# A long convolution by transforms, then token mixing: another pitch for x in SBUF, joint spectrum products, and two copies on another engine

## The chip, the cores and the metric

The kernel runs on one core of a Trainium2 chip. A core has five engines that each work through a queue of their own, in order: PE (TensorE, matrix products; its weight loads are listed apart as PEld), DVE (VectorE), ACT (ScalarE), POOL (GpSimd) and SP (SyncE, here only DMA issues). They meet through semaphores. SBUF is the on-chip memory of 128 partitions, PSUM holds the results of PE, and 16 DMA engines move data between SBUF and the device memory. The metric is the device time of one execution in microseconds (us).

## The reference

The input x has 8 batches of 5696 tokens and 128 channels. Each channel is convolved along the tokens with a filter h of full length (by a transform of twice the length), and the result goes through a mixing block.

```python
# first block: B, S, D = 8, 5696, 128
L = 2 * S
Xf = np.fft.rfft(x, n=L, axis=1)
Hf = np.fft.rfft(h, n=L, axis=0)
y = np.fft.irfft(Xf * Hf[None], n=L, axis=1)[:, :S, :]
# second block, x is now y
theta = x @ w_theta
zr, zi = x * np.cos(theta), x * np.sin(theta)
y = einsum('ts,bsd->btd', w_tok_r, zr) + einsum('ts,bsd->btd', w_tok_i, zi)
u = x + y
out = u + np.maximum(u @ w_ch, 0.0)
```

## The kernel before

The second block, the mixing with two 5696 x 5696 matrices (matmuls of L1099 and L1020, matrices streamed in by POOL at L509 and transposed by VectorE at L714), takes the larger part of the run. The change touches the first block, the transform part, lines 82 to 366.

**The transform.** The length 11392 is split as N1 x N2 = 178 x 64. Of the 178 first frequencies K1 = 90 are kept. A sequence is laid out with its NB = 89 blocks of 64 tokens on the partitions. The work goes in eight groups: a pair of batches (bp = 0 to 3, e = 0, 1 inside the pair) and a half of the channels (dh = 0, 1; HD = 64 channels). Each group passes four stages:

- Stage a (`stage_a`, L185): for each channel one matmul (L194) with the 89 x 128 slice of x as the weights (128 = two batches x 64 tokens of the block) and the table f1_t, 180 columns, as the moving operand. Four channels share one PSUM tile; a copy to SBUF follows (L201, on ScalarE; for the filter h also L199, on VectorE). 16 chunks.
- Stage b (`stage_b`, L294, with `f2`, L204): for 8 frequencies at a time the second transform (L212, 32 small matmuls), a copy of the result from PSUM to xs (L310, ScalarE), and the product with the filter's spectrum hs, which SP loads four chunks ahead (L303). The spectrum's two parts (r = 0, 1) give two VectorE instructions (L312), one into u_t and one into v_t. 12 chunks, the last with 2 frequencies. At the end of `f2` for the last chunk stand 12 further matmuls (L218), whose results are not used.
- Stage c (`stage_c`, L318): the first inverse transform, 16 chunks of 8 channels, 16 matmuls each (L328 with weights from u_t, L329 from v_t), then a copy with a sign (L336 on VectorE, or L333 and L334 on ScalarE).
- Stage d (`stage_d`, L339): the last inverse transform, 7 chunks (six of 10 of the 64 token positions, one of 4) of L351 matmuls, then a copy to yt (L354, ScalarE), which SP stores.

**The order.** The instructions are written out in one order, and each engine takes its own in that order. `woven` sorts the chunks of several lists by a position between 0 and 1. For each group g there are two such stretches: stage c of g woven with stage a of g + 1, where stage a lies in the first 0.35 (g even) or 0.55 (g odd); then stage b of g + 1 woven with stage d of g.

**Buffers.** All PSUM tiles of the transform come from one pool of four (`psum`, L97). xs has two buffers, hs four, and x16, u_t, v_t, the result of stage a (a_), of stage c (g_) and yt have one each. u_t and v_t also hold the raw h and the filter's spectrum before group 0.

**The load of x.** `load_x` (L124) loads a pair of batches, float32 to float16, in 16 DMAs from POOL: 2 batches x 4 quarters of the 64 positions x the partitions 0 to 79 and 80 to 88. The first call stands in the setup, among the tables that POOL prepares (L150, L152). The others stand at the end of stage a's list for dh = 1 (`next_x`): with one x16 buffer, the first DMA waits until that stage's last matmul has read the old x. At most 8 DMAs of POOL are under way at a time.

The weights of L194 are `x16[:NB, :, dh * HD + q]`: 128 elements of 2 bytes, one per (batch, position), whose distance is the pitch of a row of x16, 128 elements or 256 B. For h the rows are 64 elements (`h16`, L118) and the distance 128 B. For u_t, v_t and g_ the 128 elements lie side by side.

Of the kernel before, what the change touches and what calls it, by code (L numbers as in the profile page):

```python
# [12 lines left out]
F16 = mybir.dt.float16  # L13
add = mybir.AluOpType.add
mult = mybir.AluOpType.mult
AF = mybir.ActivationFunctionType
# [6 lines left out]
def kernel(  # L23
# [10 lines left out]
    nc = tc.nc  # L34
    B, S, D = x.shape
    assert D == 128
    P = 128
# [39 lines left out]
    N2 = 64  # L77
    N1 = NF // N2
    NB = S // N2
    K1 = N1 // 2 + 1  # L80
    CK = 8
    HD = D // 2
    EN = N2 // 2 + 1
    WARM = 12
    assert N1 * N2 == NF and NB * N2 == S and NB % 2 == 1 and K1 <= P
    CHK = [(c0, min(CK, K1 - c0)) for c0 in range(0, K1, CK)]
    NCK = len(CHK)
    CN = 10
    CHN = [(c0, min(CN, N2 - c0)) for c0 in range(0, N2, CN)]
    UVW = 2 * HD * K1  # L90
# [6 lines left out]
    def psum():  # L97
        return fp.tile([P, 2, 512], F32, tag="ps", name="ps")
# [3 lines left out]
    def pool(name, bufs, stack, **kw):  # L102
        return stack.enter_context(tc.tile_pool(name=name, bufs=bufs, **kw))
# [3 lines left out]
    fx = pool("fft_x", 1, xin)  # L107
    NE, WB, BT = 9, 6 * 4 * CJ * 64, 7 * 1024
    keep = pool("keep", 1, ctx, side="right")
    fc = pool("fft_c", 1, conv, side="right")  # L110
# [1 line left out]
    s1 = pool("set_1", 1, setup, side="right")  # L112
    s2 = pool("set_2", 2, setup, side="right")

    u_t = fc.tile([P, UVW + P], F16)
    v_t = fc.tile([P, UVW + P], F16)
    uv = [t[:, :UVW].rearrange("p (e d k) -> p e d k", e=2, k=K1) for t in (u_t, v_t)]
    h16 = s1.tile([P, 2, N2, HD], F16)  # L118
    for p0, p1 in ((0, 80), (80, NB)):
        nc.gpsimd.dma_start(u_t[p0:p1, :N2 * D],  # L120
                            bass.AP(tensor=h.tensor, offset=h.offset + p0 * N2 * D,
                                    ap=[[N2 * D, p1 - p0], [1, N2 * D]]))

    def load_x(bp):  # L124
        x16 = fx.tile([P, 2, N2, D], F16, tag="x16", name="x16")
        for e in range(2):
            src = x[2 * bp + e]
            for n0 in range(0, N2, 16):
                for p0, p1 in ((0, 80), (80, NB)):
                    nc.gpsimd.dma_start(  # L130
                        x16[p0:p1, e, n0:n0 + 16, :].rearrange("p n d -> p (n d)"),
                        bass.AP(tensor=src.tensor, offset=src.offset + (p0 * N2 + n0) * D,
                                ap=[[N2 * D, p1 - p0], [1, 16 * D]]))
        return x16

    lane = fc.tile([P, 2], F32)
# [6 lines left out]
    def turns_of(pattern, base, lanes, m, per, quarter=None):  # L143

        n = 1
        for _, c in pattern:
            n *= c
        t = s2.tile([P, 11 * NB], F32, tag="turn", name="turn")[:m, :n]
        k = s2.tile([P, 11 * NB], F32, tag="whole", name="whole")[:m, :n]
        nc.gpsimd.iota(k, pattern=pattern, base=base, channel_multiplier=0,  # L150
                       allow_small_or_imprecise_dtypes=True)
        nc.gpsimd.tensor_scalar(t, k, lanes, 1.0 / per, op0=mult, op1=mult)  # L152
        if quarter is not None:
            quarter(t)
        nc.vector.tensor_scalar(k, t, MAGIC, None, op0=add)
        nc.vector.scalar_tensor_tensor(t, k, MAGIC, t, op0=ALU.subtract, op1=ALU.subtract)
        return t, k
# [12 lines left out]
    t, k = turns_of([[1, K1]], 0, lane[:NB, 1:2], NB, N1)  # L170
# [33 lines left out]
    def f2(a_st, c):  # L204
# [11 lines left out]
        if c == NCK - 1:  # L216
            for n in range(WARM):
                nc.tensor.matmul(ps[:, n % 2, ck * HD:ck * HD + 384], w_t2[:, 2, :P],  # L218
# [11 lines left out]
    for k0 in (0, 15, 30):  # L230
        w_table(k0)
    nc.vector.tensor_copy(h16[:NB], u_t[:NB, :N2 * D].rearrange("p (n h d) -> p h n d", h=2, d=HD))
    x16s = {0: load_x(0)}
    steps, a_h = stage_a(lambda q: h16[:NB].rearrange("p h n d -> p (h n) d")[:, :, q], True)
    woven(steps, [lambda k0=k0: w_table(k0) for k0 in range(45, K1, 15)])
# [20 lines left out]

    for c in range(NCK):
        h_chunk(c)
    nc.gpsimd.memset(u_t[:, UVW:], 0.0)
    nc.gpsimd.memset(v_t[:, UVW:], 0.0)  # L260

    r_u = fc.tile([P, P], F16)
    r_v = fc.tile([P, P], F16)
# [30 lines left out]
    def stage_b(a_st, dh):  # L294

        hs_of = {}

        def load(c):
            if c >= NCK:
                return  # L300
            hs = hs_of[c] = fh.tile([P, 2, HD * CK], F16, tag="hs", name="hs")
            for e in range(2):
                nc.sync.dma_start(hs[64 * e:64 * e + 64], hf_hbm[dh, c])  # L303

        def chunk(c):
            c0, ck = CHK[c]
            hv = hs_of[c].rearrange("p r (d k) -> p r d k", k=CK)
            ps = f2(a_st, c)
            xs = fs.tile([P, 2, HD, CK], F16, tag="xs", name="xs")
            nc.scalar.activation(xs[:, :, :, :ck], ps, AF.Copy)  # L310
            for r in range(2):
                nc.vector.tensor_tensor(  # L312
                    uv[r][:, :, :, c0:c0 + ck], xs[:, :, :, :ck],
                    hv[:, r:r + 1, :, :ck].to_broadcast([P, 2, HD, ck]), op=mult)
            load(c + LEAD)
        return [lambda c=c: load(c) for c in range(LEAD)], [lambda c=c: chunk(c) for c in range(NCK)]
# [22 lines left out]
    def stage_d(st, bp, dh, then=None):  # L339
        def chunk(n0, cn):  # L340
            if n0 == 0:
                st["yt"] = fg.tile([P, NB, N2], BF16, tag="yt", name="yt")
            g_, yt = st["g"], st["yt"]
            ps = psum()
            nq = 5 if cn == CN else cn
            for j in range(cn):
                n = n0 + j
                o = ps[:, j // nq, (j % nq) * NB:(j % nq + 1) * NB]
                for ri in range(2):
                    e_ = e_t[:K1, n, ri, :] if n < EN else e_t[:K1, N2 - n, ri, ::-1]  # L350
                    nc.tensor.matmul(o, g_[:K1, ri * N2 + n, :], e_, start=(ri == 0), stop=(ri == 1))  # L351
            y_out = yt[:, :, n0:n0 + cn].rearrange("p m (a q) -> p m a q", q=nq)
            y_in = ps[:, :cn // nq, :nq * NB].rearrange("p a (q m) -> p m a q", q=nq)
            nc.scalar.activation(y_out, y_in, AF.Copy)  # L354
            if n0 + cn == N2:
                if then is not None:
                    then(yt)
                if then is not None:
                    gate = nc.gpsimd.tensor_copy(small(0, 1)[HD:HD + 1], sides["phases"][1][HD:HD + 1, 3, H - 1:H]).ins
                for e in range(2):  # L360
                    t0 = H if then else 0
                    with tc.issue_after(gate) if then else ExitStack():
                        (nc.gpsimd if then else nc.sync).dma_start(
                            yt_hbm[dh * HD:(dh + 1) * HD, 2 * bp + e, t0:],
                            yt[64 * e:64 * e + 64].rearrange("p m n -> p (m n)")[:, t0:])
        return [lambda n0=n0, cn=cn: chunk(n0, cn) for n0, cn in CHN]
# [125 lines left out]
    def small(at, n):  # L492
        return ring["all"][:, WB + BT + at:WB + BT + at + n]
# [436 lines left out]
    for i, (k, p, tt, j0, s0, nj) in enumerate(stretches):  # L930
# [38 lines left out]
        if tt is None:  # L969
# [24 lines left out]
            if end_of_pair:  # L994
# [5 lines left out]
                c, c0 = c_last  # L1000
# [161 lines left out]
```

## Time and profile before

| | us |
|---|---|
| median of three runs | 2101.3 (2100.75 to 2103.45) |
| span of the profiled execution | 2098.1 |
| busy PE, DVE, ACT, POOL | 1979.5, 1595.2, 675.3, 912.5 |
| weight loads (PEld) | 1109.4 |
| first stage a of a group, first copy | 55.3 |
| stage c of the eight groups, first VectorE copy | 90.5, 132.4, 174.5, 217.7, 259.8, 304.4, 347.7, 394.6 |
| loads of x for the second to fourth pair, first issue | 100.0, 184.8, 270.1 |

The profile is of one execution, taken by the hardware profiler; times in it are microseconds from the span's start unless marked ns. The groups view gives for each line, engine and kind of instruction: the tiles, output <- inputs with partitions x elements, the count, then the busy time and the mean of one in ns, then the engine's idle time just before and what ended most of it. The timeline gives start, duration, engine, line, and how many are merged in the row (xN). In the windows view each row is a stretch of time with each engine's busy time. PEclk is TensorE's granted clock as a share of the full one. The ends of matmuls are modelled, so that the distance of their starts says more than their duration.

### The profile page before, as it was taken

What the parts mean: (1) busy time and instruction counts of PE and PEld (TensorE: products, weight loads), DVE (VectorE), ACT (ScalarE), POOL (GpSimd) and SP (SyncE); (2) the same over time, 40 slices, a digit from 0 to 9 for tenths busy, and PEclk for the clock granted to TensorE, in tenths of its full rate; (3) what the DMA queues carried; (4) which work ended last, traced back from release to release, by engine and by line L of the source; (5) the groups of instructions that cost most, each with busy time, mean ns of one, the idle gap of its engine ahead of it and who ended that gap; (6) DMA issues with size and microseconds to landing.
All of it is one profiled execution on the core that took longest, in us unless ns stands there. A gap on an engine that the chain in (4) does not pass through costs nothing.

```text
span 2098.1 us, 41505 instructions
## 1 busy us (share of the span) xinstructions
PE 1979.5 (94%) x15688; PEld 1109.4 (53%) x15865; DVE 1595.2 (76%) x2881; ACT 675.3 (32%) x995; POOL 912.5 (43%) x1662
## 2 busy tenths in 40 slices
PE   4888999878999999999999999899999999999998
PEld 3788888754444444444444444344444444444444
DVE  7777776776878888888886766886777777777867
ACT  5887877874332333333310000011111111111111
POOL 5301010327444636354557554435354545445450
PEclk8799999989999999999999999999999999999999
DMA  7357474989989989898999989869797887879693
GB/s 144 94 137 175 123 171 121 239 243 239 179 153 179 178 175 168 171 173 177 171 175 152 154 167 284 136 107 156 127 154 132 148 142 136 154 130 155 126 155 89
DMA packets 408233, 334.97 MB, mean 160 GB/s; under 512 B 85895, under 2 KB 358407, under 8 KB 407047
## 3 DMA queue, kind: packets, MB, share of 16 engines
q0 software_dynamic: 225952, 156.72, 52.8%
q1 hardware_dynamic: 176096, 164.05, 27.3%
q10 hardware_dynamic: 5984, 11.54, 1.6%
q8 instruction: 124, 2.03, 0.4%
q14 instruction: 77, 0.63, 0.1%
HBM read 377.11 MB, written 92.49 MB: 224 GB/s over the span
## 4 chain that ended last, share of the span: by engine, by line
PE 63%; DVE 4%; DMA 2%; issue 2%; POOL 0%; ACT 0%; DVEq 0%
PE m L1099 59%; DVE c L1106 2%; DMA ring<-in_moe_w_tok_r_dram 1%; DVE b L655 1%; PE v L801 1%; PE utp L794 1%; PE m L1103 1%; DVE wt L714 1%; PE tpz L742 0%; PE theta_ps L396 0%; POOL ring L509 0%; PE m L986 0%; DMA yT<-yt_hbm 0%; PE m L1020 0%; DMA zl<-zl_hbm 0%
## 5 line engine op out<-in xcount | busy, mean ns | idle before, releaser
L509 POOL DMA_DIRECT2D ring<-in_moe_w_tok_i_dram x720 | 390.8, 557 | 653.0 <-DVE wt L714 579.6
L509 POOL DMA_DIRECT2D ring<-in_moe_w_tok_r_dram x720 | 389.0, 559 | 145.8 <-DVE wt L714 85.5
L714 DVE STREAM_TRANSPOSE wt<-ring 128x384 f32<-128x384 f32 (+2 forms) x720 | 359.3, 523 | 110.3 <-PE m L1099 70.0
L1099 PE MATMUL m<-b,wt 128*128 128x512 bf16 x1599 | 385.9, 380 | 4.1 <-DVE wt L714 1.7
L1099 PEld LDWEIGHTS <-wt 128*128 128x128 bf16 x1804 | 176.4, 98 | 219.7 <-DVE wt L714 7.8
L1106 DVE TENSOR_TENSOR c<-c,m 128x512 f32<-128x512 f32 x412 | 265.2, 669 | 0.4 <-PE m L1099 0.4
L796 ACT ACTIVATE ring<-utp 128x512 bf16<-128x512 bf16 x85 | 50.8, 597 | 582.3 <-PE utp L794 582.3
L328 PE MATMUL ps<-r_u,u_t 128*128 128x128 f16 x1024 | 126.4, 223 | 6.4 <-ACT red L419 3.0
L329 PE MATMUL ps<-r_v,v_t 128*128 128x128 f16 x1024 | 125.5, 223 | 0.4
L1020 PE MATMUL m<-b,wt 128*128 128x512 bf16 x466 | 110.2, 381 | 8.9 <-DMA b<-z_hbm 4.9
L791 ACT ACTIVATE ub<-c 128x512 bf16<-128x512 f32 x88 | 55.0, 628 | 191.5 <-DMA ring<-in_moe_w_tok_r_dram 113.0
L130 POOL DMA_DIRECT2D x<-in_x_dram x64 | 33.9, 536 | 184.9 <-PE ps L194 174.8
L328 PEld LDWEIGHTS <-u_t 128*128 128x128 f16 x1024 | 103.4, 101 | 5.5 <-DVE u_t L312 4.6
L329 PEld LDWEIGHTS <-v_t 128*128 128x128 f16 x1024 | 102.4, 100 | 4.4 <-issue 2.4
L310 ACT ACTIVATE xs<-ps 128x1024 f16<-128x1024 f32 x96 | 96.6, 1030 | 14.7 <-DVE v_t L312 6.7
L312 DVE TENSOR_TENSOR u_t<-xs,hs 128x1024 f16<-128x1024 f16 x96 | 68.6, 715 | 29.2 <-ACT xs L310 19.0
L1020 PEld LDWEIGHTS <-wt 128*128 128x128 bf16 x528 | 51.1, 99 | 69.2 <-issue 9.6
L194 PE MATMUL ps<-f_t,x 89*128 89x180 f16 x512 | 77.2, 298 | 4.0 <-ACT xs L310 2.6
L212 PEld LDWEIGHTS <-w_t 64*128 64x128 f16 x3240 | 60.8, 102 | 37.5 <-issue 24.5
L398 ACT ACTIVATE red<-theta_ps,magic 128x512 f32<-128x512 f32 (+1 forms) x46 | 31.6, 687 | 134.6 <-PE theta_ps L396 104.5
L194 PEld LDWEIGHTS <-x 89*128 89x128 f16 x512 | 70.8, 241 | 5.5 <-issue 4.5
L744 ACT ACTIVATE ring<-tpz 128x512 bf16<-128x512 bf16 (+1 forms) x46 | 27.5, 597 | 131.9 <-PE tpz L742 113.0
(2895 smaller groups left out, 3868.9 us busy)
## 6 DMA issues: line engine op xcount, KB each, us to landing
ring<-in_moe_w_tok_r_dram POOLq DMA_DIRECT2D x352, 96.0 KB, 4.5
ring<-in_moe_w_tok_i_dram POOLq DMA_DIRECT2D x352, 96.0 KB, 4.9
ring<-in_moe_w_tok_r_dram POOLq DMA_DIRECT2D x352, 80.0 KB, 4.5
ring<-in_moe_w_tok_i_dram POOLq DMA_DIRECT2D x352, 80.0 KB, 3.9
hs<-hf_hbm SPq DMA_DIRECT2D x192, 128.0 KB, 3.1
cp_hbm<-c SPq DMA_DIRECT2D x88, 256.0 KB, 2.5
c<-cp_hbm SPq DMA_DIRECT2D x88, 256.0 KB, 4.4
out_dram<-c SPq DMA_DIRECT2D x88, 256.0 KB, 4.5
```

Source lines behind the costliest of these rows:

```text
L194: nc.tensor.matmul(ps[:, i // 2, (i % 2) * 2 * K1:(i % 2 + 1) * 2 * K1], lhs(q + i), f1_t[:NB], start=True, stop=True)
L212: nc.tensor.matmul(ps[:, e, j * HD:(j + 1) * HD], w_t2[rows, c0 + j, N2 * (1 - ri):N2 * (3 - ri)], a_st["a"][rows, ri * K1 + c0 + j, :], s ...
L310: nc.scalar.activation(xs[:, :, :, :ck], ps, AF.Copy)
L312: nc.vector.tensor_tensor(uv[r][:, :, :, c0:c0 + ck], xs[:, :, :, :ck], hv[:, r:r + 1, :, :ck].to_broadcast([P, 2, HD, ck]), op=mult)
L328: nc.tensor.matmul(o, u_t[:, at:at + P], r_u, start=True, stop=False)
L329: nc.tensor.matmul(o, v_t[:, at:at + P], r_v, start=False, stop=True)
L509: nc.gpsimd.dma_start(wb[32 * i:32 * i + 32, :ng, :nj * 64], bass.AP(tensor=a.tensor, offset=a.offset + row0 * S + p * H + i * QR + j0 * 6 ...
L714: nc.vector.transpose(wt.rearrange("p j t r -> p (j t r)").bitcast(F32).rearrange("p (j g t) -> p g j t", j=TJ, g=4)[:, :ng, :nj], wb[:, : ...
L791: nc.scalar.activation(ub[:m].rearrange("p b d -> p (b d)"), c[:m], AF.Copy)
L1020: nc.tensor.matmul(ms[n // 2 * 2 + h], a[n][:, j, :, r], bts_of[p][jj][n % 2 * 2 + h][:, r, :], start=(n % 2 == 0 and jj == 0 and r == 0), ...
L1099: nc.tensor.matmul(ms[q], a[q][:, j, :, r], bts[jj][q][:, r, :], start=(jj == 0 and r == 0), stop=(jj == NJ - 1 and r == 1 and q not in left))
L1106: nc.vector.tensor_tensor(c, z, ms[q], op=op)
```

## The change

Three edits:

- The rows of x16 get a pitch XP = 132 elements (264 B) of which 128 are used. The DMAs write them as 16 pieces of 128 elements per partition where they wrote one run of 2048.
- u_t and v_t become two parts of one tile uv_t, u_t in front, v_t behind it, without the 128 spare columns between them. The two products of a chunk with 8 frequencies become one instruction over (r, e, channel, frequency) in which xs is repeated over r and the spectrum over e. The last chunk, with 2 frequencies, keeps two instructions. One of two memsets of spare columns goes.
- In stage d the copies of the first and the fourth of seven chunks are VectorE's (`tensor_copy`) where they were ScalarE's.

```diff
+    XP = D + 4
...
-    u_t = fc.tile([P, UVW + P], F16)
-    v_t = fc.tile([P, UVW + P], F16)
-    uv = [t[:, :UVW].rearrange("p (e d k) -> p e d k", e=2, k=K1) for t in (u_t, v_t)]
+    uv_t = fc.tile([P, 2 * UVW + P], F16)
+    u_t, v_t = uv_t[:, :UVW + P], uv_t[:, UVW:]
+    uv = uv_t[:, :2 * UVW].rearrange("p (r e d k) -> p (r e) d k", r=2, e=2, k=K1)
...
-        x16 = fx.tile([P, 2, N2, D], F16, tag="x16", name="x16")
+        x16 = fx.tile([P, 2, N2, XP], F16, tag="x16", name="x16")
...
-                        x16[p0:p1, e, n0:n0 + 16, :].rearrange("p n d -> p (n d)"),
+                        x16[p0:p1, e, n0:n0 + 16, :D],
                         bass.AP(tensor=src.tensor, offset=src.offset + (p0 * N2 + n0) * D,
-                                ap=[[N2 * D, p1 - p0], [1, 16 * D]]))
+                                ap=[[N2 * D, p1 - p0], [D, 16], [1, D]]))
...
-    nc.gpsimd.memset(u_t[:, UVW:], 0.0)
-    nc.gpsimd.memset(v_t[:, UVW:], 0.0)
+    nc.gpsimd.memset(uv_t[:, 2 * UVW:], 0.0)
...
-            for r in range(2):
+            if ck == CK:
                 nc.vector.tensor_tensor(
-                    uv[r][:, :, :, c0:c0 + ck], xs[:, :, :, :ck],
+                    uv[:, :, :, c0:c0 + ck],
+                    xs.rearrange("p e d k -> p e (d k)").unsqueeze(1).to_broadcast([P, 2, 2, HD * CK]),
+                    hv.rearrange("p r d k -> p r (d k)").unsqueeze(2).to_broadcast([P, 2, 2, HD * CK]), op=mult)
+            for r in range(2 if ck < CK else 0):
+                nc.vector.tensor_tensor(
+                    uv[:, 2 * r:2 * r + 2, :, c0:c0 + ck], xs[:, :, :, :ck],
                     hv[:, r:r + 1, :, :ck].to_broadcast([P, 2, HD, ck]), op=mult)
...
-            nc.scalar.activation(y_out, y_in, AF.Copy)
+            if n0 in (0, 3 * CN):
+                nc.vector.tensor_copy(y_out, y_in)
+            else:
+                nc.scalar.activation(y_out, y_in, AF.Copy)
```

The instructions of TensorE stay the same in kind and order. On VectorE 176 products become 88, and 16 copies are added; in a group its order is: product of chunk 0, copy of the first chunk, products of chunks 1 to 5, copy of the fourth chunk, products of chunks 6 to 10 and the two of chunk 11. On POOL the number of DMAs stays at 64 for x.

## The prediction

> **What bounds the kernel now.** I read the chain of waits and the slices first, to see which part of the run the change can reach. The span is 2098.1 us in the profiled execution; the median of the runs is 2101.3, so I add 3.2 us to every sum made inside the span. The changed lines run only in the transform part, the first fifth.
>
> ```profile
> PE 63%; DVE 4%; DMA 2%; issue 2%; POOL 0%; ACT 0%; DVEq 0%
> PE   4888999878999999999999999899999999999998
> DMA  7357474989989989898999989869797887879693
> ```
>
> From about 525 us on PE is busy in nearly every slice with the mixing matmuls of L1099, none of them touched. Those matmuls follow the transform, and the weight ring is filled only from 385 us on, so an earlier end of the transform should move all that follows forward by as much.
>
> Inside the transform each of the eight groups (b, half of d) takes 42 to 44 us and has two stages. The windows view cuts one group into them (columns: PE, PEld, DVE, ACT, POOL busy with instruction counts, granted clock, DMA share, GB/s):
>
> ```profile
> 173.20:196.60 23.40, 22.51 (x336) 22.06 (x337) 15.27 (x13) 15.17 (x23) 8.30 (x16) 0.93 0.82 174
> 196.60:214.20 17.60, 13.64 (x467) 11.96 (x468) 13.99 (x22) 14.86 (x18) 0.00 (x0) 1.00 0.77 187
> ```
>
> In the first, stage c of this group woven with stage a of the next, PE works 22.5 of 23.4 us; DVE and ACT have 8 us to spare. In the second, stage b of the next group with stage d of this one, no engine is full; ACT (14.9) and DVE (14.0) alternate with PE in a chain with few buffers. The groups view prices the steps:
>
> ```profile
> L328 PEld LDWEIGHTS <-u_t 128*128 128x128 f16 x1024 | 103.4, 101 | 5.5 <-DVE u_t L312 4.6
> L194 PEld LDWEIGHTS <-x 89*128 89x128 f16 x512 | 70.8, 241 | 5.5 <-issue 4.5
> L310 ACT ACTIVATE xs<-ps 128x1024 f16<-128x1024 f32 x96 | 96.6, 1030 | 14.7 <-DVE v_t L312 6.7
> L312 DVE TENSOR_TENSOR u_t<-xs,hs 128x1024 f16<-128x1024 f16 x96 | 68.6, 715 | 29.2 <-ACT xs L310 19.0
> ```
>
> A weight load whose columns lie side by side takes 101 ns, one of x with columns 256 B apart 241 ns. The timeline shows what that does to PE and, at the seam of two groups, to VectorE:
>
> ```profile
> 171.15 1.12 PE L194 MATMUL ps<-f_t,x 89*128 89x180 f16 x8 [0.23 <-ACT xs L310]
> 168.46 1.29 DVE L312 TENSOR_TENSOR u_t<-xs,hs 128x1024 f16<-128x1024 f16 x1
> 169.06 1.24 DVE L312 TENSOR_TENSOR v_t<-xs,hs 128x1024 f16<-128x1024 f16 x1
> 170.28 1.90 DVE L312 TENSOR_TENSOR u_t<-xs,hs 128x1024 f16<-128x1024 f16 x1
> 386.56 0.69 DVE L312 TENSOR_TENSOR u_t<-xs,hs 128x1024 f16<-128x1024 f16 x1
> ```
>
> Eight matmuls of stage a in 1.12 us, less the last one's 0.27, are some 0.12 to 0.13 us apart (other bursts give 0.13). The products of L312 take 0.69 us, but 1.2 to 1.9 while PE loads x (from 168.8 on); in the last group's seam, where no stage a follows, they stay at 0.69.
>
> **The pitch of x: matmuls.** Stage c gives the floor: 110.22 - 108.82 is 1.40 us for the 25 starts between, 0.056 us for 128 columns, so 180 columns stream in 0.079. The weights at 264 B are not in the trace. Bounds: no gain (0.13), full gain (0.079, loads hidden as those of u_t are). The nearest row is the load of h, columns 128 B apart, 174 ns, so the pitch matters; 264 B is no power of two, and I take 0.085. That is 0.045 x 64 = 2.9 us per group where PE is the bound. Seven groups have stage a beside c. In three it is spread over 0.55 of c: 2.9 each. In four it is packed in 0.35, where ACT's 16 copies (16 in 10.79 us when alone) need 10.8 of the 14.3 us that they take now; I take 2.0. Sum 3 x 2.9 + 4 x 2.0 = **-17** (0 to -23).
>
> [...]
>
> **The seam.** Of the 2.4 us by which the three stretched products above are late, PE used part for stage a; it stood idle 0.51 + 0.23 + 0.88 = 1.6 us there. I take 0.7 for each of seven seams, **-5** (0 to -11).
>
> **One product instruction.** 88 pairs of L312 become 88 instructions of 2048 elements; the last chunk of two columns keeps two. Pairs start 0.603 us apart, the 128x256 form 0.30 apart; along that slope 2048 elements take 1.01 us, without any gain 1.21. I take 1.1. It is 0.1 x 11 per group on an engine that waits in that stage; it pays for half a copy below and I count no time for it. Cover gone, it would be up to 1.1 us per group either way. The first matmul of c now waits for the same last chunk as before.
>
> **Two copies on VectorE.** ACT's yt copy has median 0.92 us and blocks ACT 0.80 (113.69 - 112.88 to the next start). Two less give ACT 1.6 us per stage. VectorE has no such row: by L336 (1024 elements 1.13 apart) 890 take 0.98, by L199 (720 in 0.89) about 1.07 with overlap. I take 1.0. DVE then has 11 x 1.1 + 0.6 + 2.0 = 14.7 us, ACT 13.3, PE 14. The fourth copy stands behind the product of chunk 5 in VectorE's queue; chunk 9's matmuls wait for its PSUM buffer, the products of chunks 6 to 11 queue behind it, and ACT waits for them with two xs buffers. Following the order by hand with these prices, the stage ends 1.1 us earlier, not 1.6. Seven stages and 1.0 in the last d: **-8.7** (+4 to -13).
>
> **The pitch of x: transfers.** Each DMA of L130 wrote rows of 4 KB and now writes pieces of 256 B: 64 x 2 x 89 = 11392 per pair of batches. What POOL pays to issue, from the two lines nearest in count of pieces (512 and 128):
>
> ```profile
> L761 POOL DMA_DIRECT2D wl<-in_moe_w_tok_r_dram x11: 749/765/830, 1051.3 to 1173.7; - x11
> L509 POOL DMA_DIRECT2D ring<-in_moe_w_tok_r_dram x720: 532/550/615, 385.2 to 2063.2; - x180
> ```
>
> 215 ns for 384 pieces, so 1280 pieces cost some 1.2 us instead of 0.53 for each of eight DMAs, +5 us of POOL per pair. In steady state nothing else is on POOL there. At the start the tables' L150 and L152 stand behind them (x11 from 23.03 to 29.19), but the VectorE work that takes those tables begins at 35.86, so I take +1.5 (0 to 5). What the transfers take:
>
> ```profile
> 187.00:196.00 9.00, 8.79 (x180) 8.56 (x176) 7.36 (x7) 4.80 (x9) 6.07 (x12) 1.00 1.06 207
> 1142.00:1143.00 1.00, 1.00 (x7) 0.46 (x5) 0.56 (x1) 0.00 (x0) 0.30 (x2) 1.00 1.84 132
> 1963.00:1964.00 1.00, 1.00 (x6) 0.43 (x5) 0.64 (x2) 0.00 (x0) 1.00 (x3) 1.00 1.30 206
> 184.77 4.13 POOL L130 DMA_DIRECT2D x<-in_x_dram  x8 [73.10 <-PE ps L194]
> ```
>
> Row 1 is the old x load: all engines full, 207 GB/s of bytes written. Row 2 is the burst of L761's 128-byte pieces, 132 GB/s: 16 x 128 / 132 = 15.5 ns a piece and engine. Row 3 is the ring's 640 and 768 bytes, 206 GB/s: about 55 ns for 704. Between them 256 B cost 24 ns, so a pair takes 11392 x 24 / 16 = 17 us instead of 14. The upper end multiplies by the overlap that the DMA share shows (1.84 and 1.30): 28.5 and 71, so 38 ns, 27 us.
> The load starts at 184.8 when stage a has read the old x, and the next stage a starts at 214.3, 29.5 us later; with c and the seam shorter, 27. The stage's own loads (hs, 24 x 128 KB, at about 200 GB/s some 15 us for two stages, half of it inside) share the engines: 1 + 17 + 7 = 25 us, just in time. I take +1 for each of three loads, as hs comes later to stage b: **+4.5** with the start (0 to +30).
>
> [...]
>
> **Sum.** -17 - 5 - 8.7 + 4.5 = -26. 2098.1 - 26 = 2072 in the span, **2075** as median.
>
> **The rivals.**
> The late x (slower). If a piece of 256 B, whose start is now at odd multiples of 8 B, costs 45 ns, a load takes 1 + 32 + 7 = 40 us against 27; PE, in order, stands 13 us at L194 with c behind it, three times: 2075 + 39 = **2114**. It outweighs the gain from 9 us per load on, 39 ns a piece. For it: engines are full today, and 38 ns is the upper end. Against: the 132 GB/s burst of smaller pieces. 0.17.
> The pitch does nothing for the load of weights: both the -17 and the -5 go, 2101.3 - 8.7 + 4.5 = **2097**. For it: the matmuls of h, whose weights load in 174 ns, start 0.15 us apart all the same (15 in 2.50). Against: they are the first of the run and last 356 ns each where those of x last 292, so something else slows them. 0.12.
> VectorE becomes the bound of b and d (14.7 of some 16 us, copies in the way): the -8.7 goes, **2084**. For it: ACT already waits 6.7 us for L312. 0.10.
> The joint instruction falls to the rate of L336 (2.26 us): 11 x 1.05 more on VectorE, some 8 us in eight stages, 2075 + 64 = **2139**. Against: both inputs are still 16 bit and contiguous inside. 0.03.
>
> **How the numbers follow.** The forecast has 0.58. Its own range is 2056 to 2092. All gains at their ends give -47, 2054; weak gains (pace 0.11: 0.02 x 64 x 7 = 9, no gain at seam and copies, +8 for transfers) give 2100. The range 2054 to 2102 takes in the second and third rivals and leaves the late x and the slow rate out, 0.2. A measurement tells 0.2%, 4 us, from no change. Faster: 0.58 + 0.10 + half and more of the pitch rival, 0.74. Same 0.07. Slower 0.19.
>
> **What would show it.** Right: weight loads of x near 100 to 180 ns, starts of L194 under 0.1 us apart, c with a some 20 us long; no product stretched at the seam; 88 products of 1.1 us; yt copies of 1.0 us on DVE; x landed before its stage a. Wrong: POOL or DMA as the releaser of PE at L194 around 130, 215 and 300 us; loads of x still at 240 ns; a product of 2 us. The granted clock can blur it: it falls to 0.50 for some us after several seams, and where PE stands less this may go either way by 1.7 us a time.

## The result, and the profile after

The changed kernel takes 2090.0 us (median of four runs, 2087.5 to 2091.0) against 2101.2 (2100.8 to 2103.5): a ratio of 0.9941, 95% interval 0.9927 to 0.9955. It is 11 us faster where 26 were forecast. The profiled execution has a span of 2088.6 us, 9.5 less than before.

What the three edits were to do is there. The groups view, shapes kept apart (mean ns of one behind the busy time):

```profile
L195 PEld LDWEIGHTS <-x 89*128 89x128 f16 x512 | 46.1, 159 | 4.3 <-issue 3.7
L312 DVE TENSOR_TENSOR uv_t<-xs,hs 128x2048 f16<-128x2048 f16 x88 | 105.6, 1224 | 34.9 <-ACT xs L310 20.1 <-DMA hs<-hf_hbm 14.4
L360 DVE CAST yt<-ps 128x890 bf16<-128x890 f32 x16 | 17.2, 1078 | 0.0
```

Weight loads of x take 159 ns (241 before), 88 joint products 1.22 us, the copies on VectorE 1.08. No product is stretched any more: the longest of the 88 takes 1.243 us. One wait has grown: VectorE stands 14.4 us for the spectrum hs, 8.4 before.

I measured each stage c on PE from its first matmul of u_t to its last of v_t, and the stretch between two of them, which is stage b with d and the seam ("b/d" from here on):

| us | before | after |
|---|---|---|
| start of the first c | 88.4 | 87.4 |
| seven stages c, sum | 153.3 | 136.6 |
| four b/d without a load of x | 20.7, 20.8, 21.2, 20.3 | 19.8, 18.8, 18.5, 19.7 |
| three b/d beside a load of x | 20.6, 21.1, 22.5 | 23.2, 24.1, 26.6 |
| end of the last c | 419.5 | 406.1 |

Stage c gave 16.7 us and the undisturbed b/d 6.1, but the three b/d beside a load took 9.7 back. The windows view of c, b/d beside a load, c, and b/d without one (columns as before: PE, PEld, DVE, ACT, POOL busy, granted clock, DMA share, GB/s):

```profile
169.20:189.40 20.20, 19.15 (x310) 18.35 (x312) 13.34 (x12) 13.69 (x22) 8.98 (x12) 1.00 1.15 179
189.40:213.50 24.10, 17.99 (x512) 15.98 (x513) 17.06 (x16) 15.40 (x19) 3.00 (x4) 0.86 1.23 167
213.50:232.30 18.80, 18.80 (x313) 18.53 (x313) 13.56 (x12) 15.40 (x24) 0.00 (x0) 1.00 0.45 119
232.30:251.10 18.80, 16.10 (x517) 13.98 (x516) 16.75 (x16) 16.23 (x21) 0.00 (x0) 1.00 0.43 129
```

Rows two and four hold the same work. Beside the load the stage is 5.3 us longer; of the engines with work in it only PE is busy clearly longer, 1.9 us, at a clock of 0.86. Inside it, PE's timeline:

```profile
193.72 1.11 PE L213 MATMUL ps<-a__3343,w_t 64*128 64x64 f16 x64
198.80 1.20 PE L356 MATMUL ps<-e_t,g__3368 90*128 90x89 f16 x20 [3.97 <-issue]
199.93 1.89 PE L213 MATMUL ps<-a__3343,w_t 64*128 64x64 f16 x64
201.75 1.48 PE L356 MATMUL ps<-e_t,g__3368 90*128 90x89 f16 x20
203.16 0.53 PE L213 MATMUL ps<-a__3343,w_t 64*128 64x64 f16 x24
204.99 0.29 PE L213 MATMUL ps<-a__3343,w_t 64*128 64x64 f16 x8 [1.30 <-issue]
```

PE stands for 4.0 us and is released by "issue", that is by no semaphore that the profile shows; then 64 matmuls of L213 take 1.89 us where they took 1.11. The windows around it:

```profile
194.80:198.80 4.00, 0.03 (x3) 0.01 (x1) 2.30 (x2) 2.24 (x3) 0.00 (x0) 1.00 1.84 173
198.80:200.00 1.20, 1.20 (x24) 1.06 (x26) 0.00 (x0) 0.00 (x0) 0.00 (x0) 0.77 1.96 182
200.00:203.40 3.40, 3.40 (x101) 3.24 (x102) 1.73 (x2) 2.85 (x3) 0.00 (x0) 0.58 1.15 231
```

Here the clock is still whole while PE stands and falls at 199.5, when PE has work again; beside the first and the third load it falls at 114.1 and 281.4, while PE still stands (until 116.4 and 282.3). So two questions: what holds PE, and what part the edits have in it. In the same stretch VectorE's product at 200.15 waits 2.8 us for hs, which made hs the first suspect.

### The profile page after: what moved, and what is told of

It is laid out like the page before. It is cut to its first block, busy times and chain, and to the rows that moved or that the text cites. A ratio compares the mean times of both kernels' runs of the same rounds, so it can differ in the third digit from the quotient of the medians.

```text
span 2088.6 us, 41598 instructions
## 1 busy us (share of the span) xinstructions
PE 1970.4 (94%) x15865; PEld 1084.7 (52%) x15865; DVE 1589.4 (76%) x2809; ACT 646.7 (31%) x979; POOL 916.2 (44%) x1661
## 3 DMA queue, kind: packets, MB, share of 16 engines
q1 hardware_dynamic: 176096, 164.05, 27.3%
## 4 chain that ended last, share of the span: by engine, by line
PE 65%; DVE 3%; DMA 2%; issue 1%; POOL 0%; ACT 0%; DVEq 0%; POOLq 0%
PE m L1107 61%; DMA ring<-in_moe_w_tok_r_dram 2%; DVE c L1114 1%; DVE b L663 1%; PE utp L802 1%; PE v L809 1%; PE m L1111 1%; DVE wt L722 1%; PE tpz L750 0%; PE theta_ps L404 0%; POOL ring L517 0%; PE m L994 0%; PE m L1028 0%; DMA zl<-zl_hbm 0%; DMA wl<-in_moe_w_tok_i_dram 0%
## 5 line engine op out<-in xcount | busy, mean ns | idle before, releaser
L1107 PE MATMUL m<-b,wt 128*128 128x512 bf16 x1640 | 391.4, 381 | 2.0 <-DVE wt L722 1.7
L312 DVE TENSOR_TENSOR uv_t<-xs,hs 128x2048 f16<-128x2048 f16 x88 | 105.6, 1224 | 34.9 <-ACT xs L310 20.1
L333 PE MATMUL ps<-r_u,uv_t 128*128 128x128 f16 x1024 | 122.4, 220 | 10.2 <-ACT red L427 3.5
L1028 PE MATMUL m<-b,wt 128*128 128x512 bf16 x480 | 113.9, 387 | 10.8 <-DMA b<-z_hbm 6.3
L131 POOL DMA_DIRECT2D x<-in_x_dram x64 | 48.5, 766 | 167.6 <-PE ps L195 156.7
L334 PE MATMUL ps<-r_v,uv_t 128*128 128x128 f16 x1024 | 121.5, 220 | 0.2
L334 PEld LDWEIGHTS <-uv_t 128*128 128x128 f16 x1024 | 100.3, 98 | 9.3 <-issue 8.1
L333 PEld LDWEIGHTS <-uv_t 128*128 128x128 f16 x1024 | 100.5, 98 | 5.2 <-DVE uv_t L317 3.8
L310 ACT ACTIVATE xs<-ps 128x1024 f16<-128x1024 f32 x96 | 91.2, 986 | 33.1 <-PE ps L213 24.1
L213 PEld LDWEIGHTS <-w_t 64*128 64x128 f16 x3240 | 64.4, 105 | 42.2 <-issue 25.9
L428 ACT ACTIVATE mag<-mag,half_pi 128x512 f32<-128x512 f32 (+1 forms) x90 | 65.0, 723 | 0.0
L663 DVE TENSOR_TENSOR b<-b 128x1024 bf16<-128x1024 bf16 x100 | 61.5, 685 | 0.0
```

The costliest lines, as they stand in the source:

```text
L213: nc.tensor.matmul(ps[:, e, j * HD:(j + 1) * HD], w_t2[rows, c0 + j, N2 * (1 - ri):N2 * (3 - ri)], a_st["a"][rows, ri * K1 + c0 + j, :], s ...
L312: nc.vector.tensor_tensor(uv[:, :, :, c0:c0 + ck], xs.rearrange("p e d k -> p e (d k)").unsqueeze(1).to_broadcast([P, 2, 2, HD * CK]), hv. ...
L333: nc.tensor.matmul(o, u_t[:, at:at + P], r_u, start=True, stop=False)
L334: nc.tensor.matmul(o, v_t[:, at:at + P], r_v, start=False, stop=True)
L428: nc.scalar.activation(mag, mag, AF.Sin, bias=half_pi[:m], scale=-TWO_PI)
L663: return [lambda f=f, x=x: f(*x) for f, x in ((nc.vector.tensor_sub, (bt[M3], b12, b22)), (nc.vector.tensor_sub, (bt[M4], b21, b11)), (nc. ...
```

## Experiments

Ratios are to the kernel before, with 95% intervals. "Theory one" is the forecast's own mechanism with a larger price: x's pieces delay the loads of hs, and stage b waits for these.

**One edit at a time.** The pitch alone; then the joint product and the copies without the pitch; then the copies alone.

```diff
+    XP = D + 4                                 # pitch_only: before, with the diff's two edits of x16
```

> The kernel before with rows of x at 264 B, nothing else. Theory one (the pitch pays in stage c as forecast, its transfers in 256-B pieces cost about 5 us per later load): the seven stages c are 15 to 18 us shorter together, the three stages b/d beside a load 3 to 5 us longer each than before, the other three 0 to 1 us shorter; 2101 - 17 - 3 + 15 + 1 = about 2097. Rival (the pitch costs little, the stalls of the changed kernel come from the copies on VectorE): 2101 - 17 - 5 + 4 = about 2083, and the b/d beside a load keep their 20.6 to 22.5 us.

```diff
-        x16 = fx.tile([P, 2, N2, XP], F16, ...)
+        x16 = fx.tile([P, 2, N2, D], F16, ...)  # no_pitch: after, with before's DMAs
```

> The changed kernel with the rows of x back at 256 B and 4-KB runs (joint product and the two copies on VectorE stay). Theory one: the b/d stages are 1 to 2 us shorter each than before, with and without a load beside them, stages c as before; 2101 - 9 = about 2092, so that the pitch by itself is worth only some 2 us in the changed kernel. Rival (copies and joint product put VectorE in the way): the b/d stages beside a load are 2 to 4 us longer than before, 2105 or more.

```diff
+            if n0 in (0, 3 * CN):               # copies_only: before, with this edit alone
+                nc.vector.tensor_copy(y_out, y_in)
```

> The kernel before with the two copies of stage d on VectorE alone; the products stay two instructions per chunk. Theory A (copies and joint product each do little, as PE's own work of 15.4 us is nearly all of a b/d stage): b/d stages 0 to 0.8 us shorter, 2097 to 2102. Theory B (the copies gain what was forecast and the joint product loses it again): b/d 1 to 1.5 us shorter each, 2090 to 2094. Theory C (without the joint product VectorE has too much to do): b/d 0.5 us or more longer, 2104 to 2110.

Measured: pitch alone 2090.7 us, 0.9949 (0.9935 to 0.9963), the same as all three edits; without the pitch 2101.7, 1.0004 (0.9994 to 1.0014); copies alone 2101.9, 1.0005 (0.9994 to 1.0016). With the pitch alone the seven c take 137.1 us, b/d beside a load 26.1, 24.1, 26.1 and the others 19.1, 19.0, 19.7, 21.5. So both the gain and the stalls belong to the pitch; my expectation for the kernel without it (2092) missed by 10 us, and the pitch alone lay between its two (2097 and 2083). Without the pitch twelve joint products take 1.6 to 2.5 us, with the pitch alone a single product is stretched; so the stretching belongs to the weight loads at 256 B, too. The windows of one undisturbed b/d, before and without the pitch, show how little came of the copies:

```profile
237.80:258.50 20.70, 17.19 (x517) 14.96 (x509) 17.07 (x25) 18.80 (x23) 0.00 (x0) 1.00 0.46 131
```

```profile
238.90:259.00 20.10, 16.85 (x516) 14.64 (x516) 18.47 (x16) 17.45 (x21) 0.00 (x0) 1.00 0.45 134
```

ScalarE has 1.4 us less to do, VectorE 1.4 more, and the stage with the same matmuls is 0.6 us shorter (0.4 on average over the four without a load). VectorE is now the fullest engine, 18.5 of 20.1 us, and PE is busy 16.9. That these two keep the gain small is argued from the busy times; no run isolates it.

**Is it hs?** In the three groups beside a load, eight of twelve loads of hs are left out.

```diff
...                                         # again: the three groups beside a load
+            if again and c >= LEAD:
+                hs_of[c] = hs_of[c - LEAD]
+                return
```

> The changed kernel, but in the three groups whose stage b runs beside a load of x only the first four chunks load their spectrum; the later eight multiply with those four again, so that eight of twelve loads of hs are left out there and x's load is as it was. Theory one (x's pieces hold up the spectrum's loads, and stage b waits for these): the b/d stages beside a load fall from 23.1, 24.1 and 26.6 us to 18.5 to 20, 11 to 18 us in all, about 2076. Rival (x itself comes late, or VectorE is the bound): the stages keep 23 to 26 us, or get shorter by under 2 us each; 2085 to 2090.

Measured: 2089.4 us, 0.9949 (0.9933 to 0.9965), and 26.8, 24.3, 27.0 us for the three b/d. Theory one falls: with two thirds of hs gone, nothing is gained. PE's timeline in the third of them shows what the stall is:

```profile
276.89 0.52 PE L213 MATMUL ps<-a__5296,w_t 64*128 64x64 f16 x23 [0.77 <-issue]
277.35 1.02 PE L359 MATMUL ps<-e_t,g__5321 90*128 90x89 f16 x20
278.30 1.11 PE L213 MATMUL ps<-a__5296,w_t 64*128 64x64 f16 x64
279.34 1.02 PE L359 MATMUL ps<-e_t,g__5321 90*128 90x89 f16 x20
280.29 0.20 PE L213 MATMUL ps<-a__5296,w_t 64*128 64x64 f16 x1
285.28 1.88 PE L213 MATMUL ps<-a__5296,w_t 64*128 64x64 f16 x63 [4.80 <-issue]
287.10 1.68 PE L359 MATMUL ps<-e_t,g__5321 90*128 90x89 f16 x20
288.71 1.03 PE L213 MATMUL ps<-a__5296,w_t 64*128 64x64 f16 x32
289.68 1.16 PE L359 MATMUL ps<-e_t,g__5321 90*128 90x89 f16 x13
291.20 0.71 PE L359 MATMUL ps<-e_t,g__5321 90*128 90x89 f16 x7 [0.37 <-issue]
```

Count the matmuls from one stop to the next: 23 + 20 + 64 + 20 + 1 = 128, and 63 + 20 + 32 + 13 = 128; in the changed kernel above, from 198.80 to 204.99, 20 + 64 + 20 + 24 = 128. The stops have nothing to do with the program's chunks (one splits a group of 64 after its first matmul); they come every 128 matmuls with their 128 weight loads. The page of the changed kernel says what has that size, in the busy times and in the table of DMA queues (packets, MB, share):

```profile
PE 1970.4 (94%) x15865; PEld 1084.7 (52%) x15865; DVE 1589.4 (76%) x2809; ACT 646.7 (31%) x979; POOL 916.2 (44%) x1661
q8 instruction: 124, 2.03, 0.4%
```

2 x 15865 instructions in 124 packets are 256 for each packet of 16 KB. PE's own program is fetched in such blocks over the same DMA engines, and PE runs dry when a block comes late. The trace also has the packets of this queue one by one, and they agree. In the undisturbed b/d from 232.3 us a packet starts 0.2 to 1.1 us after PE has begun a block, and the block after it is the one it brings. In the stretch above PE begins blocks at 192.0 and 198.8 us, but the packets run from 195.76 to 197.20 and from 202.33 to 203.58: they start 3.8 and 3.5 us after the block, and PE goes on 1.6 and 1.4 us after they have landed. All eight such stops in the three b/d beside a load end 1.3 to 1.8 us after the landing of a packet. In b/d PE uses one up in 3.6 us where nothing disturbs it (276.89 to 280.49), in stage c in some 8 (310 matmuls and 312 loads in 20.2 us). That is theory two: x's pieces hold up these blocks; PE runs dry, and the clock falls behind it. The kernel before has it too, smaller. Its waits of PE in the same b/d (total us, times, longest):

```profile
PE ps L212 <- issue: 2.2, 2, 1.1
```

Over the three b/d beside a load PE waits for issue 3.1 + 2.2 + 2.7 = 8.0 us before and 5.1 + 5.3 + 5.5 = 15.9 after; the clock is at half there for 6.8 us before (all in the third; after waits of 3.1 and 2.2 us it stayed whole) and 6.8 + 6.8 + 13.7 = 27.3 after.

**How small are the pieces allowed to be?** The kernel before, with the rows of x at 256 B as they were, but written in 256-B pieces (each DMA takes every second row), and in 512-B pieces (every second pair of rows).

```diff
-                                ap=[[N2 * D, p1 - p0], [1, 16 * D]]))
+                                ap=[[N2 * D, p1 - p0], [2 * D, 16], [1, D]]))      # pieces_at_128
+                                ap=[[N2 * D, p1 - p0], [4 * D, 8], [1, 2 * D]]))   # pieces_512
```

> The kernel before, its rows of x at 256 B, but each DMA of x writes the even or the odd ones of 32 rows: 16 pieces of 256 B per partition in place of one run of 4 KB, as many pieces as the changed kernel has, at multiples of 256 B. Theory one (the count of pieces costs, not their place): the load's pieces take as long as in the changed kernel (about 680 pieces per us), b/d beside a load 2.5 to 4 us longer than before; 2101 + 8 to 15 = 2109 to 2116. Rival (the odd starts of 264-B rows cost, as partial lines): pieces at multiples of 256 B move at 850 per us or more, and the time is 2101 to 2105.

> The kernel before, rows of x at 256 B, each DMA of x in pieces of 512 B (every second pair of rows of a block of 32), half as many pieces as at 256 B (2117.9) and four times as many as... 4-KB runs have one run per partition where this has eight. Theory P (the engines' time goes by the piece, about 23.5 ns each up to some size): a load takes 5696 x 40 to 47 ns / 16 = 14 to 17 us as before, since 512 B at 200 GB/s take that anyhow; 2100 to 2106. Theory Q (a write in pieces costs in proportion to their number over the whole range): half of the 17.7 us that the 256-B pieces cost, 2107 to 2112.

Measured: 256-B pieces 2117.9 us, 1.0073 (1.0055 to 1.0092); 512-B pieces 2104.7, 1.0024 (1.0014 to 1.0034). Two b/d beside a load, with 256-B pieces:

```profile
112.30:137.70 25.40, 20.09 (x513) 17.69 (x512) 16.75 (x25) 18.55 (x22) 3.00 (x4) 0.80 1.21 170
202.20:228.70 26.50, 19.42 (x513) 17.20 (x512) 17.02 (x25) 18.49 (x21) 3.01 (x4) 0.81 1.21 164
```

Each is 5 us longer than before, without any pitch; so it is the pieces. Where they start does not matter: in their densest 5 us 682 per us land at multiples of 256 B, 679 in the changed kernel, that is 16 engines / 680 = 23.5 ns per piece and engine. A 512-B piece takes 42.5 ns (376 per us). As transfers the load is 11392 x 23.5 / 16 = 16.7 us, 15.1 and (712 packets at 312 ns) 13.9 us in the three forms: 3 us apart where the kernel's times are 17 apart. With 512-B pieces the three b/d beside a load are 24.8, 22.8 and 23.0 us long. The packets of PE's instructions that run into the pieces there start 2.0 to 3.8 us after PE has begun a block with 4-KB runs (three packets), 2.7 to 3.3 with 512-B pieces (six, and a seventh after 1.2) and 3.5 to 4.4 in the changed kernel (six); all others in the b/d of these kernels start within 2.2. PE's waits for issue are 8.0, 10.1 and 15.9 us, and the clock is at half for 6.8, 13.7 and 27.3. By the byte the engines' time is little different, 23.5 ns being little over half of 42.5; but the kernel does pay much more for the step from 512 to 256 B (a ratio of 1.0024 to 1.0073) than for that from 4 KB to 512 (1 to 1.0024).

**What a load costs in all.** The three later loads are left out (all pairs work on the first pair's x): in the changed kernel, in the one before, and with the pitch alone.

```diff
-                x16s[bp + 1] = load_x(bp + 1)
+                x16s[bp + 1] = x16s[0]
```

> The changed kernel without the loads of x for the second to fourth pair: all four pairs work on the first pair's x, everything else as it was. Theory two (formed after the last runs: x's pieces hold up the 16-KB blocks of PE's own instructions on the DMA engines, PE runs dry for 5 us beside each load, and the granted clock falls to a half after it): the b/d stages that had a load fall from 23 to 27 us to the 18.5 to 19.8 of the others, PE's idle time put down to issue there from 5.1-5.5 us to under 1; 2090 - 12 to 17 = 2073 to 2078. Rival (the stalls are not the load's): 2085 to 2090.

> The kernel before without the loads of x for the second to fourth pair. Theory two: PE's idle time by issue in the stages that had a load (3.1, 2.2, 2.7 us) goes, but these stages were no longer than the others (20.6, 21.1, 22.5 against 20.7, 20.8, 21.1), so that the time stays within 4 us of 2101. With the run above: a load in 4-KB runs costs at most 1 us, one in 256-B pieces 4 to 6. Rival (the load costs as much in either form): 2085 to 2090 here as well.

> The pitch alone, without the later loads of x (all pairs use the first pair's x). Beside the changed kernel without these loads (2072.7) it shows what joint product and copies are worth where no load disturbs b/d. Theory one of the forecast (1.25 us a stage, 8.7 in all): 2080 to 2083. Theory A (PE's own work is nearly all of b/d, the two edits are worth little): 2071 to 2076. By theory two the loads cost 12 to 17 us here too: 2090.7 less that.

Measured: 2072.7 us, 0.9865 (0.9847 to 0.9883), for the changed kernel; 2104.7, 1.0016 (1.0003 to 1.0028), for the one before; 2075.3, 0.9892 (0.9875 to 0.9908), for the pitch alone. The stretches of the changed kernel that had a load:

```profile
107.50:126.00 18.50, 15.51 (x513) 13.56 (x513) 16.60 (x16) 15.93 (x20) 0.00 (x0) 1.00 0.46 136
183.70:202.70 19.00, 15.73 (x513) 13.47 (x512) 16.67 (x16) 16.25 (x21) 0.00 (x0) 1.00 0.41 123
261.10:280.50 19.40, 16.82 (x513) 14.87 (x512) 16.67 (x16) 15.57 (x20) 0.00 (x0) 0.91 0.42 125
```

73.9 us have become 56.9, and the kernel's time fell by 2090.0 - 2072.7 = 17.3. So three loads in 256-B pieces cost 17 us. In 4-KB runs they cost nothing: without them the old kernel is even 3 us slower (interval 0.6 to 5.9). Its b/d gain 3.7 us in sum, but its seven c lose 4.7 to half clock at their seams; why the clock falls there more often is not settled. Joint product and copies are worth 2.6 us of median here (the two intervals overlap), 3.7 us over seven b/d, 0.5 each.

**Does it go by number or by place?** Half of each later load left out (only the first batch of a pair is loaded), so that the pieces were to end before stage c does; in the trace they end 1.6 to 1.9 us into b/d, where those of a whole load reach some 15 us into it.

```diff
...                                         # the pairs share one x16
-        for e in range(2):
+        for e in range(1 if bp else 2):
```

> The changed kernel with half of each later load left out: only the first batch of a pair is loaded (5696 pieces instead of 11392), the second stays that of the first pair. The pieces then take some 8.4 us and end before stage c does. Theory two (the price comes from the pieces that lie beside b/d, where PE runs dry): nearly all of the 17.7 us that the loads cost goes, b/d 18.5 to 20 us, 2072 to 2077. Rival (the price goes with the number of pieces): half of it stays, 2080 to 2083.

Measured: 2078.1 us, 0.9884 (0.9866 to 0.9902), between the two expectations: 12 of the 17 us are gone with half the pieces. Two of the b/d:

```profile
107.50:126.80 19.30, 15.79 (x513) 13.53 (x512) 16.55 (x16) 16.55 (x21) 0.00 (x0) 1.00 0.49 138
267.00:287.80 20.80, 15.81 (x514) 13.58 (x512) 16.64 (x16) 17.06 (x21) 0.00 (x0) 0.99 0.51 130
```

They are nearly as without a load, with PE's waits for issue at 1.1, 0.3 and 1.9 us. What is left shows in them (60.1 us for 56.9) and in stage c, three of which are 1 to 3 us longer than in the changed kernel. So most of the price, not all, is the place beside b/d: by number alone half of it, some 9 us, would have stayed, and 5 did.

**Can it be had without the price?** Three ways to spread or move the load, all with the same pieces. First, fewer DMAs under way at a time, each waiting for the fourth or the second one before it:

```diff
+                    if bp and len(xd) > 4:      # or 2
+                        tc.add_manual_dep(xd[-1].ins, xd[-5].ins.name, ...)
```

> The changed kernel, but each DMA of a later load of x starts only when the fourth one before it has landed, so that at most two of the large ones (80 partitions, 1280 pieces, some 1.9 us of all engines each) stand in the queues where four could. Theory two: the blocks of PE's instructions wait behind half as much, PE's idle time by issue beside a load falls from 5.3 to some 2 to 3 us, the stages from 24.6 to 21 or 22 on average; 2080 to 2085. Rival (what counts is the share of the engines' time that x takes, not how much stands queued): no change, 2088 to 2092.

> As the run before, with one large DMA of x under way at a time (each waits for the second one before it). A large one takes some 1.9 us of transfer and about 2 us until it has landed and the next is issued: 8 of them 31 to 35 us against 27 us from the last read of the old x to the next stage a. Theory two: PE's idle time by issue beside a load falls under 1.5 us, but x itself may be 4 to 8 us late, which shows as a wait of the first matmuls of stage a for a DMA; 2078 to 2095, by how late it is. Rival: idle time by issue as in the changed kernel, 5 us, and the late x on top; 2100 or more.

Measured: 2092.8 us, 0.9961 (0.9947 to 0.9975), with waits for issue of 6.0, 1.9 and 6.1 us; and 2148.5, 1.0222 (1.0205 to 1.0239), where PE waits for x itself 19 to 21 us a load and for issue still 3.7, 2.7 and 5.1. How much of x stands queued is not what counts, then, as far as these two kernels go; a block is late even with a single large DMA of x under way. By what rule the engines choose between the queues no run here shows.

Second, a load in two parts, the later one waiting for a product of stage b. In the first two kernels it waits nearly until the next c, and stage a is moved back there; a third moves stage a alone; in the last two the load only pauses.

```diff
+        load_x(bp + 1, slice(0, 5))             # after stage a, as now
...
+        load_x(bp + 1, slice(5, 8))             # waits for chunk 10 (split5), 4 (pause5)
...
-(a_, 0.0, 0.35 if dh == 0 else 0.55)
+(a_, 0.0, 0.35) if dh == 0 else (a_, 0.4, 0.95) # split5, late_a
```

> The changed kernel with the later loads of x kept out of b/d: the first five of the eight row quarters are issued as now, at the end of the old x's stage a in the middle of stage c; the last three wait for the product of chunk 10 of stage b, so that they fall into the next stage c, and the stage a that reads them is moved in that c from 0 to 0.55 to 0.4 to 0.95. As many pieces as in the changed kernel. Theory two (a load costs 17 us in all only because it lies beside b/d, where PE uses up its instructions fastest): PE's idle time by issue in the three stages falls from 5.3 us to under 2, the stages to 19 to 21 us, the half clock there goes; the c with the late stage a may be 1 to 3 us longer; 2076 to 2083. Rival (the pieces cost the same wherever they lie): PE is held up in c instead, by 4 to 6 us a load; 2087 to 2093.

> As the run before with the parts four and four; the second waits for the product of chunk 8, so that its first 2 or 3 us lie in the end of b/d, and stage a is at 0.45 to 1.0 of c. Theory two: 2076 to 2086, PE's idle time by issue in b/d up to 2 us from the pieces at its end; stage a later in c, up to 3 us more at the seam than in the run before. Rival: 2087 to 2093.

> The changed kernel with stage a moved as in the split load (0.4 to 0.95 of c for the first half of a pair's channels), the load of x as it was: the control for that move. Theory two: the load still lies beside b/d, idle time by issue 5 us, b/d 23 to 27 us; within 4 us of the changed kernel's 2090. Rival (it is the place of stage a that pays): 2076 to 2083 as in the split load.

> The changed kernel; the first five of eight row quarters of a later load are issued as now, the last three wait for the product of chunk 4 of stage b, some 7 us into b/d; stage a stays where it was. The load pauses where PE ran dry (the block of instructions that came late was the second of b/d). Theory two: idle time by issue falls from 5.3 to 2 to 3 us and the half clock with it, if x is still in time: 2080 to 2086; if x comes late at the seam, which shows as a wait of L195's matmuls for a DMA, up to 2100. Rival: no change, 2087 to 2093.

> As the run before with six and two, the two waiting for chunk 6, some 10 us into b/d. Theory two: the same, 2080 to 2086; the first part runs 2 us further into b/d (idle time by issue 1 us more), the second has 4 us of transfers in the last 7 us. Rival: 2087 to 2093.

Measured: split5 2122.0 us, 1.0106 (1.0092 to 1.012); split4 2123.4, 1.0113 (1.0098 to 1.0129); late_a 2101.8, 1.0008 (0.9998 to 1.0018); pause5 2105.7, 1.0025 (1.0012 to 1.0037); pause6 2110.2, 1.0052 (1.0032 to 1.0072). All lose, and the reason is one my expectations left out: the engines have no room elsewhere. In split5 the b/d beside the first part are 19.2, 20.0 and 19.2 us long with 1.5, 0.4 and 1.4 us of issue, as theory two has it, but x then comes 8 to 10 us late in the next c, where the stores of yt (two of 712 KB) use the engines; and stage a late in c makes that c 3.5 us longer by itself (22.3 us in late_a). The pause shows the exchange most clearly; PE's waits in the first b/d of pause5:

```profile
PE ps L200 <- DMA x<-in_x_dram: 8.2, 1, 8.2
...
PE ps L218 <- issue: 0.2, 1, 0.2
```

The stall by issue is gone (0.2 for 5.1), and x itself is 8.2 us late. Beside the second load it is 0.9 and 9.1 us, beside the third 5.0 and 3.9, so the pause did not always keep the stall away.

Third, an earlier start of the load, by letting VectorE take five copies of the stage a before it and ScalarE six of stage c's:

```diff
+            if both and q % 8 or q in some:     # some = range(4, HD, 12) for dh = 1
...
-(a_, 0.0, 0.35 if dh == 0 else 0.55)
+(a_, 0.0, 0.25 if dh == 0 else 0.55)
```

> The changed kernel with the loads issued earlier: in the stages a whose end frees x, five of sixteen copies go to VectorE and the list lies in 0 to 0.25 of c, and of stage c's copies ScalarE takes six in place of four. ScalarE's copies of that stage a then take 8.5 us instead of 12.3. Theory two: the load starts 1.5 to 2.5 us earlier and ends as much earlier; a stall of 5 us and the half clock behind it shrink, 2 to 4 us for each of three loads, unless c gets longer by VectorE's work (19 us of 19): 2080 to 2090. Rival: no change or slower by the copies, 2088 to 2098.

Measured: 2089.2 us, 0.9937 (0.9919 to 0.9954), the changed kernel within the error. The three b/d are 24.8, 24.5 and 24.6 us; three stages c are 0.5 to 1.6 us shorter, but the four b/d without a load are 0.3 to 2.3 us longer than in the changed kernel. No version here beats the changed kernel measurably.

## Why the prediction was half right

The sum failed in one term and was too high in another.

- **Pitch, matmuls (-17): right.** The seven c are 16.7 us shorter. A burst of twelve of its matmuls takes 1.14 us, starts some 0.08 apart (0.085 taken). The weights of x load in 159 ns where they took 241.
- **Seam (-5): right in kind, low in size.** Undisturbed b/d with the pitch alone are 19.1, 19.0 and 19.7 us against 20.7, 20.8 and 21.2, 1.6 each for 0.7 (the fourth is longer, 21.5 against 20.3, with 1.7 us of waits for issue and 3.4 at half clock); in the kernels without loads 0.8 each.
- **Joint product (0): right.** Two in 2.36 us on VectorE, so 1.13 to 1.2 each for the 1.1 taken.
- **Two copies on VectorE (-8.7): too high.** Alone, 0 (interval -1.3 to +3.4 us); 2.6 without loads. The step "the stage ends 1.1 us earlier" followed ScalarE's chain and did not hold PE's own 16 to 17 us and VectorE's rise against it; the b/d got 0.4 to 0.5 us shorter. In undisturbed b/d VectorE is busy 16.75 of 18.80 us (14.7 forecast for it): this is the third rival, the only one of the four that fits in part, though that VectorE is the bound was not tested.
- **Transfers (+4.5): the step that failed.** The start cost nothing (first c 1.0 us earlier; +1.5 taken). The rate of 24 ns per 256-B piece was right (23.5), and so was "just in time": the pieces of a load landed over 24 to 25 us, and stage a did not wait for x. What failed is "+1 for each of three loads, as hs comes later to stage b". hs does come later, but the runs show that it does not matter; PE's instruction blocks come later too, PE waits 5 us for them beside each load, and half clock follows for 7 to 14 us. Measured, the three loads cost 17 us instead of 3.
- **The clock** was named as a blur of 1.7 us a time; it was a part of the price itself, 27 us at half beside the three loads.
- **The rivals.** The late x did not happen in the changed kernel (and only every second row, not each, starts at an odd multiple of 8 B), though pause and split made it happen on the other side of the same shortage; loads of weights did get faster; the joint instruction kept its rate.

Against the forecast's 26, then, in the two profiled executions: the three b/d beside loads are 12 us off (+9.7 for -2.4); the undisturbed ones about 1; the start -2.5. The last 4 are lost after the transform: its end came 13.4 us earlier, the end of the span 9.5. A stretch at half clock near 575 us is part of it. Single executions of the changed kernel differ by 3.4 us, and in the kernel without loads the shift was kept (29.0 at the end of the last c, 29.7 at the end), so I do not put it down to the edits.

## What to carry to other kernels

Before a transfer is cut into small pieces, ask not only whether it is in time but what else rides on the same DMA engines, PE's own instructions included: a stage of short matmuls here uses a block of 256 instructions in 3.6 us, and a wait put down to "issue" that returned after every 128 matmuls was that block coming late. Such a stall can cost twice, once while PE stands and once in the half clock behind it: beside the three loads here 15.9 us of waits and 27.3 us at half clock. And when an engine is relieved, look first how busy the engine that bounds the stage is by itself: copies moved off ScalarE shortened a b/d by 0.4 to 0.5 us where 1.1 was forecast, with PE busy 16.1 and VectorE 16.75 of its 18.8 us.

## What the runs showed of the hardware

- PE's program comes in packets of 16 KB, 256 instructions, over a queue of its own ("instruction"), and these are held up by other transfers: in an undisturbed b/d a packet started 0.2 to 1.1 us after PE had begun a block, beside x's 256-B pieces up to 4.4; beside 4-KB runs PE's longest stop in a b/d was 2.2, 1.1 and 2.7 us, beside 256-B pieces 3.7 to 4.8. With each DMA of x waiting for the fourth one before it PE still waited 6.0, 1.9 and 6.1 us for issue, for the second one 3.7, 2.7 and 5.1 (5.1, 5.3 and 5.5 in the changed kernel).
- Weight loads of 89 x 128 elements take 173 ns in the mean at a distance of 128 B, 241 at 256 B and 159 at 264 B. VectorE's joint products took up to 2.52 us beside the loads at 256 B, and none over 1.243 in the changed kernel.
- The time of a DMA engine per piece was 23.5 ns for 256 B, 42.5 for 512 B, 312 for 4 KB; it did not depend on whether the pieces start at multiples of 256 B (682 per us at multiples, 679 in the changed kernel).
- Beside the three loads of the changed kernel the granted clock fell to half in stretches of 3.4 us or multiples (3.4, 6.8, 13.7), late in a stall or after it: it was 1.00 while PE stood from 194.8 to 198.8 and 0.58 in the busy 3.4 us from 200.0. The falls (114.1, 199.5, 206.3, 281.4) lie whole multiples of 3.41 us apart; in the 3.41 us before them PE was busy for 1.85, 0.66, 2.11 and 0.62 us. What sets off a fall no run here shows.
